# Two-layer MLP after attention, fp32 by split weights: part 2's first layer with one PSUM bank for each product and the sums on VectorE

## The chip, the cores and the metric

One Trainium2 chip, one of its cores. The metric is the device time of one execution in microseconds (us). It is given as the median of several runs; the profile shows one execution.

## What is computed

Attention with keys and values pooled by eight, then two MLPs in sequence on the 4608 tokens. The change is in the second MLP ("part 2"), whose first layer goes from 512 to 2048 units and whose second goes back to 512:

```python
def _moe_ref(x, w1, w2, w3, w_out):
    h = np.maximum(np.maximum(x @ w1, x @ w2), x @ w3)
    return h @ w_out

def _moe2_ref(x, w_in, w_out):
    h = np.maximum(x @ w_in, 0.0)
    return h * h @ w_out
```

All tensors are float32. TensorE multiplies them as pairs of parts (a high part in `float32r` and the rest), with three matmuls for each product of tiles (`PARTS`: high by high, high by rest, rest by high).

## The kernel before

Part 1 (attention and the first MLP) runs to about 764 us of the span and writes its result y to DRAM. Part 2 runs over nine blocks of 512 tokens (`for j in range(NB2)`), and in each over four groups of hidden units (`for gr in range(NG)`, 512 units each).

Both layers of part 2 are done with seven block products in place of eight, as in Strassen's scheme (Winograd's form): the operands are cut in 2 by 2 blocks, sums and differences of blocks are multiplied, and the four result blocks are sums of products. For the first layer the seven combinations of y are made and split once for each block (`mix_y`, `split_y`, L604 to L622, in the sequence of `ORDER`, L624), and the seven combinations of weights lie in SBUF (`wi2s`). `product(bank, j, gr, m)` (L639) issues the 12 matmuls of product m, 128x256 each, into one PSUM bank (6 for each half of the units, `u`). `moe2_in` (L664) forms the four unit tiles `c[h, half]` (128x512 each) from the products, and squares their positive part. With c00, c01, c10, c11 for c[0, 0] and so on, and m1 to m7 for the products, the result is

```
c00 = m1 + m2          c01 = m1 + m6 + m5 + m3
c10 = m1 + m6 + m7 + m4  c11 = m1 + m6 + m7 + m5
```

Before, three banks serve a group. Bank x takes m1, then m6, m7 and m4 on top of it, so that TensorE makes the running sums; after m1, m6 and m7 ScalarE copies the running sum out (`partial_sum`, L678), and the next product may add to the bank only when that copy has read it. m5 goes to bank y (and m3 later on top of it), m2 to bank z; VectorE adds these to the copies (`complete`, L680: an add at L656 and a square at L662). Only c10 is taken straight from bank x by ScalarE, with Relu (L698) and Square (L699).

The second layer (`moe2_out`, L765) takes the unit tiles as its left operands. For each of its products ScalarE makes the high part `g` of an operand (L124), VectorE the rest (L125), and TensorE issues 12 matmuls (L779): 8 with the high part, then 4 with the rest. They add up in five banks accA, accB, accD, accE and accF over the whole block. Groups 0 and 1 of a block have 4 such products ("outs"), groups 2 and 3 have 10 (`OUT`). When a bank is complete, `evacuate` (L737) takes it out: accA by a ScalarE copy into `o` (L748), the others by VectorE adds. An out's weights (`wo2s`, 512 KB) are fetched from DRAM shortly before, in five buffers (`wo_p`), each fetch issued by SyncE when an earlier out has released a buffer.

PSUM has eight banks: the five of `acc_ps` and three that the pool `mm_ps` hands out, the earliest released first. The order on each engine is fixed when the kernel is built: the framework's scheduler lays the instructions of all engines out by its own estimates of durations, so that outs of one group are placed between products of the next. Each engine then runs its list strictly in that order.

Of the kernel before, what the change touches and what calls it, by code (L numbers as in the profile page):

```python
# [14 lines left out]
AF = mybir.ActivationFunctionType  # L15
# [69 lines left out]
def attention_moe_kernel(ctx: ExitStack, tc: tile.TileContext, q, k, v, vn, w1, w2, w3, wo1, wi2, wo2, out):  # L85
    nc = tc.nc
# [501 lines left out]
    def shared_place(i, shape, name):  # L588
        return y_p.tile(shape, F32, tag=f"r{i}", name=name)
# [31 lines left out]
        split(y, src[m])  # L621
        src[m] = y  # L622

    ORDER = (1, 5, 6, 2, 7, 4, 3)  # L624
    early = [functools.partial(load_y, 0), functools.partial(mix_y, 0)]
    early.append(functools.partial(fetch_in, 0, w2_p))
    early += [functools.partial(split_y, 0, m) for m in ORDER]
    for i, f in enumerate(early):
# [10 lines left out]
    def product(bank, j, gr, m, first=False):  # L639

        i, o = PLACES[m]
        for u in range(2):
            n = 0
            for kk in range(2):
                for a, c in PARTS:
                    nc.tensor.matmul(  # L646
                        bank[:, u * HT : (u + 1) * HT],
                        lhsT=wi2_t[2 * gr + u][i][:, a, o + kk * P : o + (kk + 1) * P],
                        rhs=y_t[j][m][:, c, kk],
                        start=(first and u == 0 and n == 0), stop=(u == 1 and n == 5),  # L650
                        skip_group_check=not first,
                    )
                    n += 1

    def add(out, in0, in1):
        nc.vector.tensor_tensor(out=out, in0=in0, in1=in1, op=ALU.add)  # L656
# [4 lines left out]
    def squared(c):  # L661
        nc.vector.scalar_tensor_tensor(out=c, in0=c, scalar=0.0, in1=c, op0=ALU.max, op1=ALU.mult)  # L662

    def moe2_in(j, gr):  # L664

        def unit(h, half):
            if half and gr < NG // 2:
                return shared_place(4 * gr + h, [P, T2], "a21")
            return c_p.tile([P, T2], F32, tag=f"c{2 * half + h}", name=f"c{2 * half + h}")

        def bank():
            return mm_ps.tile([P, T2], F32, tag="ps", name="ps")

        c = {}

        def partial_sum(h, half, ps):
            c[h, half] = unit(h, half)
            nc.scalar.activation(c[h, half], ps, AF.Copy)  # L678

        def complete(h, half, ps):  # L680
            add(c[h, half], ps, c[h, half])
            squared(c[h, half])

        x, y = bank(), bank()
        product(x, j, gr, 1, first=True)
        partial_sum(0, 0, x)
        product(y, j, gr, 5, first=True)
        product(x, j, gr, 6)
        partial_sum(0, 1, x)
        z = bank()  # L690
        product(z, j, gr, 2, first=True)
        complete(0, 0, z)
        product(x, j, gr, 7)
        partial_sum(1, 1, x)
        complete(1, 1, y)
        product(x, j, gr, 4)
        c[1, 0] = unit(1, 0)
        nc.scalar.activation(c[1, 0], x, AF.Relu)  # L698
        nc.scalar.activation(c[1, 0], c[1, 0], AF.Square)  # L699
        product(y, j, gr, 3)  # L700
        complete(0, 1, y)
        return c

    OUT = {
        False: ((1, 0), (1, 1), (7, 1), (7, 0)),
        True: ((2, 0), (4, 1), (5, 1), (6, 1), (2, 1), (3, 1), (6, 0), (4, 0), (5, 0), (3, 0)),
    }
    BANKS = {1: "A", 2: "A", 7: "B", 4: "B", 6: "D", 5: "E", 3: "F"}
    FULL = {"A": 8, "B": 8, "D": 4, "E": 4, "F": 4}
# [86 lines left out]
    for j in range(NB2):  # L796
        for gr in range(NG):
            more = j + 1 < NB2
            c = moe2_in(j, gr)

            ready = list(ORDER) if gr == NG - 1 and more else []
            for n, (m, h) in enumerate(OUT[gr >= NG // 2]):
                if n == 6 and ready:
                    mix_y(j + 1)
                if n >= 6:
                    for y in ready[2 * n - 12 : 2 * n - 10]:
                        split_y(j + 1, y)
                moe2_out(j, gr, m, h, c)
            if gr == NG - 2 and more:
                load_y(j + 1)  # L810
            nxt = j * NG + gr + 1
            if nxt < NB2 * NG:
                fetch_group(nxt % NG)
# [41 lines left out]
```

## Time and profile before

| what | value |
|---|---|
| median of 3 runs | 1520.89 us (1520.51 to 1523.3) |
| the profiled execution: its time | 1521.12 us |
| the profiled execution: its span, first to last instruction | 1519.3 us |
| mean granted TensorE clock | 0.992 of full speed |
| busy share: TensorE matmuls, VectorE, ScalarE | 97%, 62%, 49% |
| part 2 (763.9 to 1519.3 us of the span) | 755.4 us |
| one block of part 2 away from the ends (1186.38 to 1268.61) | 82.23 us, 672 matmuls |

A reader of such a profile looks first at the engine that is busy nearly all the time, then at what ends each of its pauses. In the timeline, the bracket behind a row is the idle time of the engine before it and the instruction that ended it. Matmuls overlap each other, so the "us" of a row ends after the next row has begun; the distance from start to start is what counts.

### The profile page before, as it was taken

What the parts mean: (1) busy time and instruction counts of PE and PEld (TensorE: products, weight loads), DVE (VectorE), ACT (ScalarE), POOL (GpSimd) and SP (SyncE); (2) the same over time, 40 slices, a digit from 0 to 9 for tenths busy, and PEclk for the clock granted to TensorE, in tenths of its full rate; (3) what the DMA queues carried; (4) which work ended last, traced back from release to release, by engine and by line L of the source; (5) the groups of instructions that cost most, each with busy time, mean ns of one, the idle gap of its engine ahead of it and who ended that gap; (6) DMA issues with size and microseconds to landing.
All of it is one profiled execution on the core that took longest, in us unless ns stands there. A gap on an engine that the chain in (4) does not pass through costs nothing.

```text
span 1519.3 us, 27411 instructions
## 1 busy us (share of the span) xinstructions
PE 1467.2 (97%) x10410; PEld 1438.5 (95%) x10410; DVE 946.2 (62%) x1724; ACT 742.4 (49%) x1947; POOL 178.6 (12%) x228
## 2 busy tenths in 40 slices
PE   6879999999999999999999999999999999999998
PEld 4879999999999999999999999999999999999997
DVE  5786466675675746754335757575756657575755
ACT  6785356655666556653233434343434443443432
POOL 2442022313222212321000000000000000000000
PEclk9989999999999999999999999999999999999999
DMA  6553135534444424425197656474656566665746
GB/s 211 168 178 107 54 118 164 167 98 139 160 136 160 139 89 129 132 87 181 55 356 289 215 168 248 142 253 161 231 198 212 192 222 210 214 205 170 254 125 211
DMA packets 118306, 263.93 MB, mean 174 GB/s; under 512 B 12672, under 2 KB 62848, under 8 KB 118176
## 3 DMA queue, kind: packets, MB, share of 16 engines
q1 hardware_dynamic: 111264, 252.75, 50.3%
q10 hardware_dynamic: 6912, 9.44, 1.7%
q8 instruction: 82, 1.34, 0.4%
q14 instruction: 48, 0.39, 0.1%
HBM read 213.91 MB, written 48.23 MB: 173 GB/s over the span
## 4 chain that ended last, share of the span: by engine, by line
PE 88%; DMA 5%; ACT 4%; DVE 2%; issue 1%; SPq 0%; ACTq 0%; DVEq 0%
PE ps L502 28%; PE ps L646 23%; PE ps L521 10%; PE accB L779 6%; PE accA L779 6%; PE accE L779 3%; PE accD L779 3%; PE accF L779 3%; PE sc L342 2%; DMA wo2s<-wo_dram 2%; PE tr L370 2%; ACT ss L347 1%; PE av L399 1%; PE av L398 1%; ACT c L678 1%; DMA yr<-y_dram 1%
## 5 line engine op out<-in xcount | busy, mean ns | idle before, releaser
L502 PE MATMUL ps<-x,w 128*128 128x384 f32 x2592 | 493.6, 341 | 6.3 <-POOL w L125 4.8
L502 PEld LDWEIGHTS ps<-x,w 128*128 128x128 f32 x2592 | 451.3, 190 | 9.8 <-POOL w L125 6.4
L646 PE MATMUL ps<-y,wi2s 128*128 128x256 f32 x3024 | 388.6, 280 | 16.7 <-ACT c L678 11.1
L646 PEld LDWEIGHTS ps<-y,wi2s 128*128 128x128 f32 x3024 | 368.1, 188 | 24.0 <-ACT c L678 15.3
L521 PE MATMUL ps<-h,wo 128*128 128x384 f32 x864 | 163.2, 341 | 0.9 <-ACT ys L527 0.7
L521 PEld LDWEIGHTS ps<-h,wo 128*128 128x128 f32 x864 | 150.8, 190 | 1.7 <-ACT ys L527 0.9
L124 ACT ACTIVATE g<-c 128x512 fp32r<-128x512 f32 x144 | 90.6, 629 | 123.2 <-DVE c L662 56.7
L125 DVE TENSOR_TENSOR g<-c,g 128x512 fp32r<-128x512 f32 x144 | 99.1, 688 | 43.8 <-ACT g L124 43.1
L779 PE MATMUL accA<-wo2s,g 128*128 128x256 f32 x864 | 124.6, 283 | 1.7 <-DMA wo2s<-wo_dram 1.7
L510 DVE TENSOR_TENSOR hm<-ps,hm 128x384 f32<-128x384 f32 x144 | 79.5, 552 | 75.0 <-PE ps L502 72.7
L779 PE MATMUL accB<-wo2s,g 128*128 128x256 f32 x864 | 119.3, 283 | 0.2 <-DMA wo2s<-wo_dram 0.2
L656 DVE TENSOR_TENSOR c<-ps,c 128x512 f32<-128x512 f32 x72 | 49.5, 687 | 106.0 <-ACT c L678 90.3
L779 PEld LDWEIGHTS accA<-wo2s,g 128*128 128x128 f32 x864 | 112.3, 190 | 2.1 <-ACT g L124 1.2
L779 PEld LDWEIGHTS accB<-wo2s,g 128*128 128x128 f32 x864 | 110.4, 191 | 0.4 <-issue 0.4
L347 ACT ACTIVATE ss<-sc,st 128x72 f32<-128x72 f32 (+1 forms) x320 | 97.9, 320 | 15.1 <-DVE st L344 14.1
L353 POOL TENSOR_TENSOR ss<-ss,st 128x432 f32<-128x432 f32 (+1 forms) x64 | 56.8, 888 | 262.8 <-DVE st L352 195.9
L678 ACT ACTIVATE c<-ps 128x512 f32<-128x512 f32 x72 | 42.6, 592 | 91.5 <-PE ps L646 76.1
L656 DVE TENSOR_TENSOR a<-ps,a 128x512 f32<-128x512 f32 x36 | 24.9, 692 | 98.9 <-ACT a L678 64.5
L402 DVE TENSOR_TENSOR xf<-av,xf 64x192 f32<-64x192 f32 (+1 forms) x112 | 50.7, 453 | 48.7 <-ACT xf L401 47.1
L124 ACT ACTIVATE h<-hm 128x384 fp32r<-128x384 f32 x72 | 37.7, 523 | 73.2 <-DVE hm L510 72.6
L374 DVE TENSOR_TENSOR pt<-tr,pt 72x192 fp32r<-72x192 f32 (+1 forms) x112 | 49.7, 450 | 37.6 <-ACT pt L373 36.2
L401 ACT ACTIVATE xf<-av 64x192 f32<-64x192 f32 (+1 forms) x112 | 45.4, 405 | 54.0 <-PE av L399 39.0
(104 smaller groups left out, 2016.5 us busy)
## 6 DMA issues: line engine op xcount, KB each, us to landing
wo2s<-wo_dram SPq DMA_DIRECT2D x252, 512.0 KB, 4.6
wi2s<-wi_dram SPq DMA_DIRECT2D x24, 512.0 KB, 9.0
wraw<-in_wo_dram SPq DMA_DIRECT2D x22, 512.0 KB, 4.0
wraw<-in_w_dram SPq DMA_DIRECT2D x18, 512.0 KB, 4.2
y_dram<-ys ACTq DMA_DIRECT2D x48, 192.0 KB, 2.1
wraw<-in_wi_dram SPq DMA_DIRECT2D x16, 512.0 KB, 3.6
wi_dram<-wraw SPq DMA_DIRECT2D x16, 512.0 KB, 3.4
wo_dram<-wraw SPq DMA_DIRECT2D x64, 128.0 KB, 2.0
```

The lines of the kernel that those rows point to most:

```text
L124: nc.scalar.activation(hi, src, AF.Copy)
L125: engine.tensor_tensor(out=lo, in0=src, in1=as_f32(hi), op=ALU.subtract)
L347: nc.scalar.activation(ss[:, i, h], src[:, i, h], AF.Exp, bias=st[:, 0, i, h : h + 1], accum_out=st[:, 1, i, h : h + 1],)
L353: nc.gpsimd.tensor_tensor(out=ss, in0=ss, in1=st[:, 2].rearrange("p g (h o) -> p g h o", o=1).to_broadcast([m, g, 2, SP]), op=ALU.mult,)
L402: nc.vector.tensor_tensor(out=xf[r], in0=av[r], in1=xf[r], op=ALU.add)
L502: nc.tensor.matmul(ps, lhsT=w1_t[f, e][:, a, kk * P : (kk + 1) * P], rhs=x[kk][:, c], start=(n == 0), stop=(n == 3 * KD - 1),)
L510: nc.vector.tensor_tensor(out=hm, in0=ps, in1=hm, op=ALU.max)
L521: nc.tensor.matmul(ps, lhsT=wo1_t[kk][:, a, d * P : (d + 1) * P], rhs=hs[kk][:, c], start=(n == 0), stop=(n == 3 * KF1 - 1),)
L646: nc.tensor.matmul(bank[:, u * HT : (u + 1) * HT], lhsT=wi2_t[2 * gr + u][i][:, a, o + kk * P : o + (kk + 1) * P], rhs=y_t[j][m][:, c, kk] ...
L656: nc.vector.tensor_tensor(out=out, in0=in0, in1=in1, op=ALU.add)
L678: nc.scalar.activation(c[h, half], ps, AF.Copy)
L779: nc.tensor.matmul(bank[:, i * 256 : (i + 1) * 256], lhsT=g[:, a, u * HT + i * P : u * HT + (i + 1) * P], rhs=w[:, u, c], start=(n == 0 an ...
```

## The change

The running sums leave TensorE's banks. Each product except m3 starts in a bank of its own (m3 still goes on top of m5). ScalarE copies only m1 out; VectorE adds every other product from its bank to the unit tiles, in a chain: c01 = m6 + c00, c10 = m7 + c01, c11 = m5 + c10, then m2, m4 and m3 into c00, c10 and c01. The squares of c11 and c01 are VectorE's, those of c00 and c10 are ScalarE's, by two passes in SBUF (Relu, then Square). The products are written in the order 1, 6, 7, 5, 2, 4, 3; the parts of y are split in that order too, and out (4, 1) comes ahead of (2, 0).

```diff
-    ORDER = (1, 5, 6, 2, 7, 4, 3)
+    ORDER = (1, 6, 7, 5, 2, 4, 3)
...
+    def squared_by_scalar(c):
+        nc.scalar.activation(c, c, AF.Relu)
+        nc.scalar.activation(c, c, AF.Square)
...
-        x, y = bank(), bank()
-        product(x, j, gr, 1, first=True)
-        partial_sum(0, 0, x)
-        product(y, j, gr, 5, first=True)
-        product(x, j, gr, 6)
-        partial_sum(0, 1, x)
-        z = bank()
-        product(z, j, gr, 2, first=True)
-        complete(0, 0, z)
-        product(x, j, gr, 7)
-        partial_sum(1, 1, x)
-        complete(1, 1, y)
-        product(x, j, gr, 4)
-        c[1, 0] = unit(1, 0)
-        nc.scalar.activation(c[1, 0], x, AF.Relu)
-        nc.scalar.activation(c[1, 0], c[1, 0], AF.Square)
+        c = {(h, half): unit(h, half) for h in range(2) for half in range(2)}
+
+        def only(m):
+            ps = bank()
+            product(ps, j, gr, m, first=True)
+            return ps
+
+        nc.scalar.activation(c[0, 0], only(1), AF.Copy)
+        add(c[0, 1], only(6), c[0, 0])
+        add(c[1, 0], only(7), c[0, 1])
+        y = only(5)
+        add(c[1, 1], y, c[1, 0])
+        squared(c[1, 1])
+        add(c[0, 0], only(2), c[0, 0])
+        squared_by_scalar(c[0, 0])
+        add(c[1, 0], only(4), c[1, 0])
+        squared_by_scalar(c[1, 0])
         product(y, j, gr, 3)
-        complete(0, 1, y)
+        add(c[0, 1], y, c[0, 1])
+        squared(c[0, 1])
...
-        True: ((2, 0), (4, 1), (5, 1), (6, 1), (2, 1), (3, 1), (6, 0), (4, 0), (5, 0), (3, 0)),
+        True: ((4, 1), (2, 0), (5, 1), (6, 1), (2, 1), (3, 1), (6, 0), (4, 0), (5, 0), (3, 0)),
```

The scheduler lays out all of part 2 anew. On TensorE, the end of the products of group 1 in the third block, before: `ps_N` is a bank as the pool hands it out, `y7_` the operand of product m7, `g` that of an out.

```order
L646 MATMUL ps_10695<-y7_10464,wi2s_2_1_8541 128x256 x6
L646 MATMUL ps_10695<-y7_10464,wi2s_3_1_8549 128x256 x6
L779 MATMUL accA_10624<-wo2s_10687,g_10797 128x256 x2
L646 MATMUL ps_10695<-y4_10468,wi2s_2_1_8541 128x256 x6
L646 MATMUL ps_10695<-y4_10468,wi2s_3_1_8549 128x256 x6
L646 MATMUL ps_10696<-y3_10490,wi2s_2_3_8545 128x256 x6
L646 MATMUL ps_10696<-y3_10490,wi2s_3_3_8553 128x256 x6
```

And the same engine with the change, in the group after it in that block, from the end of the last out to the last product:

```order
L646 MATMUL ps_10967<-y7_10480,wi2s_5_1_8565 128x256 x6
L646 MATMUL ps_10981<-y5_10483,wi2s_4_2_8559 128x256 x6
L646 MATMUL ps_10981<-y5_10483,wi2s_5_2_8567 128x256 x6
L646 MATMUL ps_10996<-y2_10504,wi2s_4_0_8555 128x256 x6
L646 MATMUL ps_10996<-y2_10504,wi2s_5_0_8563 128x256 x6
L646 MATMUL ps_11012<-y4_10508,wi2s_4_1_8557 128x256 x6
L646 MATMUL ps_11012<-y4_10508,wi2s_5_1_8565 128x256 x6
L646 MATMUL ps_10981<-y3_10530,wi2s_4_3_8561 128x256 x6
L646 MATMUL ps_10981<-y3_10530,wi2s_5_3_8569 128x256 x6
```

Before, m4 adds to the bank of m7 with two matmuls in between; with the change m5, m2 and m4 have three different banks, and the bank of m5 is used again only 24 matmuls later, by m3.

On TensorE at the end of a block, around its last out into accA, before (third block into fourth):

```order
L779 MATMUL accA_10624<-wo2s_11170,g_11346 128x256 x4
L646 MATMUL ps_11488<-y5_11388,wi2s_0_2_8190 128x256 x5
L646 MATMUL ps_11488<-y5_11388,wi2s_1_2_8527 128x256 x6
L779 MATMUL accF_11070<-wo2s_11172,g_11364 128x256 x8
L779 MATMUL accD_11038<-wo2s_11174,g_11391 128x256 x8
```

And with the change, the same place:

```order
L775 MATMUL accA_10669<-wo2s_11225,g_11406 128x256 x12
L775 MATMUL accF_11125<-wo2s_11227,g_11424 128x256 x8
```

Eleven matmuls of the next block's m5 stood between the last out into accA and the next out into accF; with the change nothing stands there.

On ScalarE at that place, with the change (`o` is the copy of accA out of PSUM, `g_11424` the operand of the out into accF; before, the two stand in this order as well):

```order
L124 ACTIVATE g_11406<-c1_11239 128x512
L124 ACTIVATE y5_11471<-t5_11440 128x512
L124 ACTIVATE y7_11468<-yr_11204 128x512
L744 ACTIVATE o_11421<-accA_10669 128x512
L124 ACTIVATE g_11424<-c1_11239 128x512
L124 ACTIVATE g_11451<-s3_10897 128x512
L124 ACTIVATE g_11474<-c2_11238 128x512
```

ScalarE makes the operand of that out only after the copy of accA, which waits for the matmuls into accA.

## Rows read from the trace of the kernel before

**Rows 1.** The page's first part: engine, busy time, share of the span, instructions.

```profile
PE 1467.2 (97%) x10410; PEld 1438.5 (95%) x10410; DVE 946.2 (62%) x1724; ACT 742.4 (49%) x1947; POOL 178.6 (12%) x228
```

**Rows 2.** TensorE's waits, 763 to 1520 us: total, times, longest (us).

```profile
PE ps L646 <- ACT c L678: 11.1, 18, 1.4
PE ps L646 <- ACT a L678: 5.1, 11, 0.7
PE accA L779 <- DMA wo2s<-wo_dram: 1.7, 2, 1.0
PE accE L779 <- DMA wo2s<-wo_dram: 1.7, 1, 1.7
PE accF L779 <- ACT g L124: 1.2, 1, 1.2
```

**Rows 3.** Timeline of TensorE, one block: start, us, instruction, [idle before <-releaser].

```profile
1186.38 4.39 PE L646 MATMUL ps<-y,wi2s 128*128 128x256 f32 x36
1190.60 1.60 PE L779 MATMUL accA<-wo2s,g 128*128 128x256 f32 x12
1192.04 4.33 PE L646 MATMUL ps<-y,wi2s 128*128 128x256 f32 x36
...
1207.34 0.41 PE L779 MATMUL accA<-wo2s,g 128*128 128x256 f32 x2
1208.19 4.51 PE L646 MATMUL ps<-y,wi2s 128*128 128x256 f32 x36 [0.44 <-ACT a L678]
1212.53 1.11 PE L779 MATMUL accA<-wo2s,g 128*128 128x256 f32 x8
...
1246.63 2.40 PE L646 MATMUL ps<-y,wi2s 128*128 128x256 f32 x19
1249.71 3.09 PE L646 MATMUL ps<-y,wi2s 128*128 128x256 f32 x24 [0.69 <-ACT c L678]
1252.65 1.12 PE L779 MATMUL accB<-wo2s,g 128*128 128x256 f32 x8
...
1259.95 1.47 PE L646 MATMUL ps<-y,wi2s 128*128 128x256 f32 x11
1261.33 1.21 PE L779 MATMUL accF<-wo2s,g 128*128 128x256 f32 x8
1262.37 1.12 PE L779 MATMUL accD<-wo2s,g 128*128 128x256 f32 x8
...
1268.61 4.39 PE L646 MATMUL ps<-y,wi2s 128*128 128x256 f32 x36
```

**Rows 4.** Groups by line and shape: count | busy us, mean ns | idle before.

```profile
L662 DVE SCALAR_TENSOR_TENSOR c<-c 128x512 f32<-128x512 f32 x72 | 49.7, 690 | 1.6
L656 DVE TENSOR_TENSOR c<-ps,c 128x512 f32<-128x512 f32 x72 | 49.5, 687 | 106.0 <-ACT c L678 90.3 <-PE ps L646 15.5
L678 ACT ACTIVATE c<-ps 128x512 f32<-128x512 f32 x72 | 42.6, 592 | 91.5 <-PE ps L646 76.1 <-DVE g L125 15.4
L699 ACT ACTIVATE c<-c 128x512 f32<-128x512 f32 x36 | 22.6, 627 | 0.6
```

**Rows 5.** Timeline of TensorE, the last block's end.

```profile
1504.19 0.64 PE L779 MATMUL accA<-wo2s,g 128*128 128x256 f32 x4
1506.03 1.21 PE L779 MATMUL accF<-wo2s,g 128*128 128x256 f32 x8 [1.20 <-ACT g L124]
1507.08 1.12 PE L779 MATMUL accD<-wo2s,g 128*128 128x256 f32 x8
```

**Rows 6.** Timeline of ScalarE at that place.

```profile
1504.87 0.60 ACT L748 ACTIVATE o<-accA 128x512 f32<-128x512 f32 x1 [4.27 <-PE accA L779]
1505.36 0.62 ACT L124 ACTIVATE g<-c 128x512 fp32r<-128x512 f32 x1
```

**Rows 7.** Stretch of a block's last group: us, busy (instructions) PE PEld DVE ACT POOL, clock, DMA.

```profile
1249.70:1271.60 21.90, 21.89 (x182) 21.78 (x183) 21.51 (x36) 11.28 (x20) 0.00 (x0) 1.00 0.55 180
```

**Rows 8.** The page's DMA issues: count, KB each, median us to landing.

```profile
wo2s<-wo_dram SPq DMA_DIRECT2D x252, 512.0 KB, 4.6
```

More of the change, by code (lines that the diff above doesn't have):

```diff
@@ L672, in bank @@
             return mm_ps.tile([P, T2], F32, tag="ps", name="ps")
[L674 to L682, printed above, removed]
-        x, y = bank(), bank()
-        product(x, j, gr, 1, first=True)
-        partial_sum(0, 0, x)
-        product(y, j, gr, 5, first=True)
-        product(x, j, gr, 6)
-        partial_sum(0, 1, x)
-        z = bank()
-        product(z, j, gr, 2, first=True)
-        complete(0, 0, z)
-        product(x, j, gr, 7)
-        partial_sum(1, 1, x)
-        complete(1, 1, y)
-        product(x, j, gr, 4)
-        c[1, 0] = unit(1, 0)
-        nc.scalar.activation(c[1, 0], x, AF.Relu)
-        nc.scalar.activation(c[1, 0], c[1, 0], AF.Square)
+        c = {(h, half): unit(h, half) for h in range(2) for half in range(2)}
[13 more added lines that the diff above has]
+        squared_by_scalar(c[1, 0])
         product(y, j, gr, 3)
-        complete(0, 1, y)
+        add(c[0, 1], y, c[0, 1])
+        squared(c[0, 1])
         return c
```

## The prediction

> **What bounds the kernel now.** I read the page's engine line first: TensorE is busy 97% of the span, VectorE 62%, ScalarE 49% [rows 1]. So the time is TensorE's, and a change can move it only through the number of matmuls, their spacing, or TensorE's pauses. The number stays: 84 matmuls for the products of a group before and after. The spacing is read from the timeline: 36 matmuls of the first layer run from 1186.38 to 1190.60, 0.117 us each, and 12 of an out from 1190.60 to 1192.04, 0.120 us each [rows 3]. That leaves the pauses, so the view that matters is the list of TensorE's waits: 29 waits for a ScalarE copy out of bank x or y (L678), 16.2 us in all (11.1 + 5.1), and a few others [rows 2].
>
> The timeline shows where they fall. In the block from 1186.38 to 1268.61 there are three: 0.44 us at 1208.19, another like it 16 us later, 0.69 us at 1249.71 [rows 3]. Each is the step m7, copy, m4 in one bank. The idle time is not all of the loss: from 1207.34 to 1212.53 stand 38 matmuls, which unhindered take 2 x 0.120 + 36 x 0.117 = 4.46 us and took 5.19. The loss is 0.73 us for an idle time of 0.44. From 1246.63 to 1252.65, 43 matmuls took 6.02 us in place of 5.04: 0.98 for 0.69. So I add 0.28 us to each wait.
>
> **What goes.** The change takes away the copies between products of one bank (L678, all but the one of m1, whose bank is free again much later). The 29 waits go: 16.2 + 29 x 0.28 = **-24.3 us**.
>
> **What is added, and where it lies.** In each of the 36 groups VectorE gets eight instructions in place of six (six adds from PSUM and two squares; before, three of each), and ScalarE five as before, of which one reads PSUM in place of four. An add from PSUM takes 687 ns on VectorE and a square in SBUF 690; a ScalarE pass takes 592 from PSUM, 627 in SBUF [rows 4]. In the stretch where VectorE is fullest it ran 36 instructions in 21.51 us, 0.60 us each [rows 7]; the added 72 cost 43 us of VectorE's time. Alone on the path it would be nearly twice the gain; I cost it at nothing, and the cover is TensorE's own work. The order rows show it: m5, m2, m4 and m3 follow each other, and each needs a bank whose last product ended at least 12 matmuls (1.4 us) before. A read that TensorE waits for with nothing to do in between cost 0.98 us with a copy of 0.59; with an add of 0.69 that is 1.08, and 12 matmuls cover it. With m3 it is 24 matmuls, and the next group's m1 and m6 find banks read one or two products earlier.
>
> Only in the first block, where weights arrive in halves and six matmuls of one product alternate with six of another (0.70 us), do six matmuls not cover it: 1.08 - 0.70 = 0.4 us, at m2 in its first three groups: **+1.2 us**.
>
> If the cover fails (VectorE late by a whole add), the next thing late is m2, 0.7 us in each group it happens.
>
> Here the Trainium skill speaks against the change (Perfetto Trace Analysis, Optimizing Scalar/DVE Operations): a VectorE instruction has some 125 ns of fixed cost on PSUM and 60 on SBUF, ScalarE 51 and 93, so reading PSUM is better left to ScalarE. By it three more PSUM reads in each of 36 groups add 3 x 36 x 65 ns = 7 us (an estimate from that page) to VectorE; the trace shows 687 against 690 ns and so no such cost on VectorE, while ScalarE's 592 against 627 agrees in sign. Either way it lies beside TensorE and the sum is the same.
>
> **A new wait at each block's end.** When accA is complete, ScalarE copies it out and only then makes the operand of the next out, into accF (front section, ScalarE's order, unchanged). Before, eleven matmuls stood between the two outs: accF's began at 1261.33, after 11 matmuls from 1259.95, and those 11 and its first 8 took 2.42 us in place of 2.25. That is 0.17 us [rows 3]. With the change nothing stands between. The last block of the kernel before shows the price, because there too the outs adjoin: 4 matmuls at 1504.19, copy at 1504.87, operand at 1505.36 [rows 6], accF at 1506.03, and 12 matmuls took 2.89 us (1504.19 to 1507.08) in place of 1.44 [rows 5]. So 1.45 us, in eight more blocks: **+11.6 us**, less the seven small ones, 7 x 0.17 = **-1.2**.
>
> **Outs' weights.** Of the three waits for `wo2s` on accA and accE [rows 2], the one on accE (1.7 us, plus 0.2 for the restart) is in the last block's end. There, all ten outs now follow the last product, and the buffer it waits for is asked for four outs ahead: **-1.9**. The two on accA (1.7 us, plus 0.4) are first outs of group 3, which ran ahead of m7 and now run after m3; I take half of 2.1, **-1.0**, as such waits can come up elsewhere.
>
> Other edits cost nothing: the order of `split_y` follows the products, and out (4, 1) goes first because c11 is the first tile complete.
>
> **Sum.** -24.3 + 1.2 + 11.6 - 1.2 - 1.9 - 1.0 = -15.6 us. The profiled execution took 1521.12 us, 0.2 above the median, of which the span is 1519.3. 1521.1 - 15.6 = **1505.5 us**.
>
> **The rivals.**
> 1. *Outs' weights set the block's end.* In the last group the outs are packed: from the last matmul of the out that releases a buffer to the first that needs the refill there are 34 to 36 matmuls, 4.1 to 4.3 us, against 4.6 us from issue to landing [rows 8]. With the wait for accA's copy in between it is 5.6, so a margin of 1 us. For it: the margin is thin, and a wait on accE reached 1.7 us [rows 2]. Against: the median holds fetches that queue behind each other. If it binds, 1.0 to 1.7 us more in eight blocks: 1513 to 1519.
> 2. *accA's copy is not waited for*, because something earlier on TensorE holds the outs apart: without the +11.6, 1493 to 1494.
> 3. *The waits only change their names.* There are still three banks, and the adds form a chain; if VectorE, strictly in order, reaches m6's or m7's add late in each group, m2 and m4 wait about what m4 waited before. 28 to 36 waits of 0.7 to 1.0 us: 1518 to 1521, no change. For it: VectorE's operands from ScalarE. Against: its idle time.
> 4. *VectorE becomes the bound at the block's end (slower).* In the last group it ran without pause from 1249.70 to 1271.60 [rows 7]. With the change some 20 VectorE instructions stand between the add of m5 (2.7 us before m3 begins) and the subtraction that accF's operand needs; 20 x 0.60 = 12.1, so it is done 9.4 us after m3's beginning. accA's last matmul ends 84 matmuls after it, at 10.0 to 10.1, and its copy holds ScalarE 0.5 more [rows 6]: 10.6. The margin is 1.2 us, two instructions. Beyond it each 0.6 us costs TensorE 0.6 in eight blocks; slower than before begins where VectorE is late by 1.2 + 18.6 / 8 = 3.5 us (18.6: the sum and the 3 us a measurement can tell). If all the 43 us came to light in place of the wait at accF, 1521 - 27 + 43 = 1537. The skill's price for PSUM reads, above, would add to this one.
>
> **How the numbers follow.** A measurement of this kernel can tell about 0.2% from no change, 3 us. Chances: forecast 0.64 (faster), rival 1 0.13 (0.11 faster, 0.02 the same), rival 2 0.09 (faster), rival 3 0.08 (the same), rival 4 0.06 (slower). Faster 0.84, the same 0.10, slower 0.06. The forecast's own terms move by a few us: the first block's +1.2 may be 3, the waits for weights 0 to -4, the 1.45 us by 0.3 in eight blocks, which gives 1500 to 1510. The range takes half of rivals 1 and 2: 1496 to 1515.
>
> **What would show it.** Right: TensorE's waits for ScalarE's copies (29 before) all but gone; accF's wait for `g` at nine places of about 1.2 us idle; a block of 81.1 us in place of 82.23; VectorE's busy time up by some 45 us, ScalarE's hardly changed. Wrong: waits of the first layer's matmuls for VectorE's adds in most groups (rival 3), waits for `wo2s` on accD, accB or accE in each block (rival 1), accF's operand following VectorE's subtraction and not accA's copy (rival 4).

## The result, and the profile after

The changed kernel takes 1504.72 us (median of 4 runs, 1503.8 to 1506.67) against 1520.7 us (4 runs, 1520.01 to 1523.3): a ratio of 0.9893, 95% interval 0.9876 to 0.9911. That is faster, by 1.1%: 16.0 us where 15.4 were forecast (1505.5 us, from the median given before). The span of the profiled execution went from 1519.3 to 1502.4 us.

The page's first part answers to [rows 1]: VectorE has 44.6 us more to do, ScalarE 3.4 more, and TensorE, with as many matmuls as before, is busy 8.7 us less, in part because some of what a wait costs stands in its busy time (the prediction read 0.98 us lost for 0.69 idle).

```profile
PE 1458.5 (97%) x10410; PEld 1435.1 (96%) x10410; DVE 990.8 (66%) x1796; ACT 745.8 (50%) x1947; POOL 179.6 (12%) x228
```

TensorE's waits in part 2, all of them (engine, line, releaser: total us, times, longest), answer to [rows 2]. Not one matmul of the first layer is left in the list. What is left is the wait for `g` at the end of each of the nine blocks, 1.2 us each, and three small entries. The last of these, put down to `y`, is by the trace's DMA records a wait for weights too: they landed 0.14 us before that out began.

```profile
PE accF L775 <- ACT g L124: 10.8, 9, 1.2
PE accE L775 <- DMA wo2s<-wo_dram: 1.5, 2, 0.9
PE accB L775 <- ACT qB L738: 0.7, 1, 0.7
PE accE L775 <- ACT y L124: 0.2, 1, 0.2
```

TensorE's timeline at a block's end (columns as in [rows 3]). The out into accF begins 2.80 us after accA's twelve matmuls begin, which take 1.44; three outs on, accE waits for its weights. In the group after it 84 matmuls of the first layer run through without a pause.

```profile
1081.70 1.12 PE L775 MATMUL accD<-wo2s,g 128*128 128x256 f32 x8
1082.66 1.60 PE L775 MATMUL accA<-wo2s,g 128*128 128x256 f32 x12
1085.46 1.22 PE L775 MATMUL accF<-wo2s,g 128*128 128x256 f32 x8 [1.21 <-ACT g L124]
1086.52 1.12 PE L775 MATMUL accD<-wo2s,g 128*128 128x256 f32 x8
1087.48 1.12 PE L775 MATMUL accB<-wo2s,g 128*128 128x256 f32 x8
1089.13 1.19 PE L775 MATMUL accE<-wo2s,g 128*128 128x256 f32 x8 [0.54 <-DMA wo2s<-wo_dram]
...
1095.62 9.85 PE L646 MATMUL ps<-y,wi2s 128*128 128x256 f32 x84
```

Why accF is late stands in ScalarE's timeline at that place: the copy `o` begins when accA is complete, and `g` comes behind it, as in [rows 6]. VectorE's subtraction for that operand (second fence) had begun at 1083.09 and was done at about 1083.8, half a microsecond before the copy began.

```profile
1083.20 0.63 ACT L124 ACTIVATE y<-yr 128x512 fp32r<-128x512 f32 x1 [1.78 <-DVE yr L610]
1084.29 0.60 ACT L744 ACTIVATE o<-accA 128x512 f32<-128x512 f32 x1 [0.46 <-PE accA L775]
1084.79 0.62 ACT L124 ACTIVATE g<-c 128x512 fp32r<-128x512 f32 x1
```

```profile
1083.09 0.69 DVE L659 TENSOR_TENSOR c<-c,s 128x512 f32<-128x512 f32 x1
```

The groups by line and shape in part 2 answer to [rows 4] (count | busy us, mean ns | idle before): VectorE's adds from PSUM are now 144 and more (other forms add into `a`), at the same 688 ns; before each of them VectorE mostly waits for TensorE, not the other way round. The first layer's copies out of a bank are down to the 36 of m1.

```profile
L656 DVE TENSOR_TENSOR c<-ps,c 128x512 f32<-128x512 f32 x144 | 97.7, 688 | 72.4 <-PE ps L646 66.1 <-ACT c L685 6.0
L662 DVE SCALAR_TENSOR_TENSOR c<-c 128x512 f32<-128x512 f32 x36 | 24.8, 688 | 0.6
L665 ACT ACTIVATE c<-c 128x512 f32<-128x512 f32 x72 | 45.1, 627 | 152.6 <-DVE c L656 151.1
L685 ACT ACTIVATE c<-ps 128x512 f32<-128x512 f32 x36 | 21.4, 594 | 25.2 <-DVE g L125 13.7 <-PE ps L646 11.6
```

**Where the 16.9 us of the two profiled spans went.** For each pause in part 2 the table takes the distance from one matmul's start to the next, less 0.118 us, and adds what the matmul behind it is late, over all 6048 matmuls of part 2.

| pause in TensorE's list | before, us | after, us | difference | forecast |
|---|---|---|---|---|
| between matmuls of the first layer, or from an out into accA to them | 26.0 | 1.6 | -24.3 | -24.3 + 1.2 |
| ahead of the first out into accF at a block's end | 2.7 | 13.2 | +10.6 | +11.6 - 1.2 |
| outs that wait for weights and the like | 5.3 | 3.6 | -1.7 | -1.9 - 1.0 |
| accB in the first block, on the copy qB | 0 | 0.95 | +0.95 | none |
| sum, with rounding | 33.9 | 19.4 | -14.5 | -15.6 |

The third row holds two waits of the first block, before the change, that [rows 2] do not show, 0.2 us idle on accB and this one:

```profile
PE accF L779 <- DMA wo2s<-wo_dram: 0.4, 1, 0.4
```

Of the 26.0 us of the first row, the 29 waits for copies are 23.9. The other 2.1 are six pauses that the forecast left out: 0.9 us once, for an operand of the next block, and five of 0.1 to 0.3.

The rest of the 16.9: 0.8 us are the other matmuls' spacing, and 1.6 us lie in part 1, in which every engine runs the same sequence of instructions in both kernels: part 2's first matmul begins at 764.1 us before and at 762.5 after. Over the twelve kernels of this study that start lay between 760.8 and 764.2, so single spans differ by up to 3 us without a change in part 1's instructions.

### The profile page after: what moved, and what is told of

Its sections match the earlier page's. It is cut to its first block, busy times and chain, and to the rows that moved or that the text cites. A ratio compares the mean times of both kernels' runs of the same rounds, so it can differ in the third digit from the quotient of the medians.

```text
span 1502.4 us, 27550 instructions
## 1 busy us (share of the span) xinstructions
PE 1458.5 (97%) x10410; PEld 1435.1 (96%) x10410; DVE 990.8 (66%) x1796; ACT 745.8 (50%) x1947; POOL 179.6 (12%) x228
## 4 chain that ended last, share of the span: by engine, by line
PE 89%; ACT 4%; DMA 3%; DVE 3%; issue 1%; ACTq 0%; SPq 0%; DVEq 0%
PE ps L502 28%; PE ps L646 23%; PE ps L521 9%; PE accA L775 7%; PE accB L775 7%; PE accE L775 4%; PE accD L775 3%; PE accF L775 3%; PE sc L342 2%; PE tr L370 2%; ACT ss L347 1%; PE av L399 1%; PE av L398 1%; DMA wo2s<-wo_dram 1%; DMA vr<-in_v_dram 1%; DMA wraw<-in_w_dram 1%
## 5 line engine op out<-in xcount | busy, mean ns | idle before, releaser
L646 PE MATMUL ps<-y,wi2s 128*128 128x256 f32 x3024 | 377.9, 280 | 0.3
L656 DVE TENSOR_TENSOR c<-ps,c 128x512 f32<-128x512 f32 x144 | 97.7, 688 | 72.4 <-PE ps L646 66.1
L665 ACT ACTIVATE c<-c 128x512 f32<-128x512 f32 x72 | 45.1, 627 | 152.6 <-DVE c L656 151.1
L775 PE MATMUL accF<-wo2s,g 128*128 128x256 f32 x432 | 61.4, 285 | 10.8 <-ACT g L124 10.8
```

What stands on the lines that cost most here:

```text
L646: nc.tensor.matmul(bank[:, u * HT : (u + 1) * HT], lhsT=wi2_t[2 * gr + u][i][:, a, o + kk * P : o + (kk + 1) * P], rhs=y_t[j][m][:, c, kk] ...
L775: nc.tensor.matmul(bank[:, i * 256 : (i + 1) * 256], lhsT=g[:, a, u * HT + i * P : u * HT + (i + 1) * P], rhs=w[:, u, c], start=(n == 0 an ...
```

## The experiments

Each ratio below is against the kernel before, in runs on one chip; "lost" is reckoned as in the table.

### Is the wait at a block's end ScalarE's order alone?

```diff
-            nc.scalar.activation(o, acc, AF.Copy)
+            nc.vector.tensor_copy(out=o, in_=acc)
```

> The changed kernel, but accA's complete sum is copied into o by VectorE and not by ScalarE, so that ScalarE makes the operand g of the out into accF without waiting for accA's last matmul. In the changed kernel that out waits nine times for g, 1.2 us idle each (10.8 in all), and about 1.45 us are lost at each place. Theory A (the wait is ScalarE's order alone): the subtraction before g is done 1.0 us earlier than the copy of accA lets g begin, so 1.0 us is won at nine places, 1504.7 - 9 = 1495.7 us, and the wait for g falls to about 0.2 us idle. Theory B (the outs' weights are late next, because the out into accE already waits in six of nine blocks and everything behind accF now moves up by 1 us): most of it comes back as waits for wo2s on accB and accE, 1501 to 1503 us, and the idle time of accE for wo2s grows from 1.5 to some 7 us. I take B as the likelier.

1503.9 us (1501.6 to 1505.26), ratio 0.989 [0.9874, 0.9907]: theory B, a microsecond above its range. The wait for `g` falls from 1.2 to 0.3 us idle, and what accF loses from 13.2 to 4.5 us; accB and accE lose 11.1 us where they lost 4.3 (the first block's accB included in both). TensorE's waits:

```profile
PE accB L775 <- DMA wo2s<-wo_dram: 3.1, 5, 1.2
PE accE L775 <- DMA wo2s<-wo_dram: 2.9, 4, 1.6
PE accF L775 <- ACT g L124: 2.1, 7, 0.3
```

The wait for weights came on accB as well as on accE, where theory B had put it. ScalarE's order was the cause of the wait for `g`, and the weights stood right behind it. The 0.3 us that is left is VectorE's: the subtraction begins at 1083.96 and `g` at 1084.74, as soon as it is done.

```profile
1083.96 0.69 DVE L659 TENSOR_TENSOR c<-c,s 128x512 f32<-128x512 f32 x1
```

```profile
1084.74 0.63 ACT L124 ACTIVATE g<-c 128x512 fp32r<-128x512 f32 x1
```

### The weights in halves, alone and with the copy moved

```diff
-    wo_p = ctx.enter_context(tc.tile_pool(name="wo_p", bufs=5, reuse_waits="tile"))
+    wo_p = ctx.enter_context(tc.tile_pool(name="wo_p", bufs=11, reuse_waits="tile"))
...
-        w = wo_p.tile([P, 2, 2, 256], F32R, tag="wo2", name="wo2s")
-        nc.sync.dma_start(out=as_f32(w), in_=wo2_dram[m, gr % 2, h])
+        pair = []
+        for u in range(2):
+            w = wo_p.tile([P, 2, 256], F32R, tag="wo2", name="wo2s")
+            nc.sync.dma_start(out=as_f32(w), in_=wo2_dram[m, gr % 2, h][:, u])
+            pair.append(w)
...
```

> The changed kernel with the outs' weights fetched as two transfers of 256 KB (one for each half of the units) into eleven buffers of half the size, in place of one of 512 KB into five; so half of an out's weights may be fetched one out earlier, and only the other half has to come after the release. In the changed kernel the out into accE starts late in six blocks, 3.2 us in all. Theory A (the time from a buffer's release to landing sets this): most of these waits go, 1501.5 to 1502.5 us. Theory B (the transfers of the block's end share a bandwidth that is used up, or their number on the queue costs as much): nothing is won, 1504 to 1507 us.

1500.59 us (1499.74 to 1502.34), ratio 0.9873 [0.9858, 0.9888]: theory A. One wait for weights is left.

```profile
PE accF L778 <- ACT g L124: 10.8, 9, 1.2
PE accE L778 <- DMA wo2s<-wo_dram: 0.8, 1, 0.8
PE accB L778 <- ACT qB L741: 0.7, 1, 0.7
```

Two things changed for these weights, worked out from SyncE's issues and the trace's records of when each transfer landed. In the changed kernel the weights of that out into accE were issued 5.6 us before the out could have begun, in seven of nine blocks (at 1082.85 in the block of the timeline above). They landed 6.15 us later there, and 5.6 to 6.6 us later in the six blocks where the out is late. With halves, in six of the nine blocks, the first half was issued 6.0 to 6.2 us ahead of the out and the second 5.6 to 5.7, and both landed after 4.3 to 5.5 us. So the first half is issued half a microsecond earlier, the second hardly, and each of them lands sooner. The page's medians, 4.2 us for 512 KB and 4.3 for 256 KB, do not show that: they rest on the 27 of 252 and the 50 of 504 transfers whose landing the page could tell. Over all of them the medians are 5.0 and 4.5 us. What each part brings, and what the larger ring (eleven halves, where five wholes are ten), was not tried apart.

> Both: weights in halves, and accA's copy on VectorE. If each of the two edits removes its own wait and nothing third is late, 1504.7 - 9 - 3.2 = 1492.5 us. If the weights stay the bound of the block's end whatever the size of the transfers, 1500 to 1503 us, as with the copy on VectorE alone.

1496.66 us (1495.67 to 1497.22), ratio 0.9845 [0.983, 0.986]. In between: with both edits accF loses 4.5 us (13.2 with the halves alone) and the weights some 4 in place of 10. So each edit works. The copy's move, which alone brought 0.8 us, brings 3.9 with the halves: accF loses 8.7 us less, the outs' weights nearly 3 more.

### The step in one bank, put back

```diff
-        add(c[0, 0], only(2), c[0, 0])
+        z = only(2)
+        add(c[0, 0], z, c[0, 0])
...
-        add(c[1, 0], only(4), c[1, 0])
+        product(z, j, gr, 4, first=True)
+        add(c[1, 0], z, c[1, 0])
```

> The changed kernel, but product m4 starts again in the bank of m2, as soon as VectorE's add has read m2, so that one of the steps product, read, product in one bank is back in each of the 36 groups, with no matmul between m2 and m4. Theory A (a read by VectorE that TensorE has to wait for costs as much as the ScalarE copies did, 0.98 us for a read of 0.59, so about 1.08 for an add of 0.69): 36 waits of the first layer's matmuls for VectorE's add, 36 x 1.08 = 39 us, 1543 us. Theory B (the scheduler and the queues hide it, and separate banks are not what the change lives on): 1505 to 1515 us.

1504.1 us (2 runs, 1502.95 and 1505.25), ratio 0.9895 [0.9875, 0.9915]: a miss by 39 us for theory A, and the sentence it rested on, that nothing would stand between m2 and m4, was wrong. The scheduler put m3 and the next group's m1 there. Its list for TensorE, in one group (the operands are y_13444 for m2, y_13470 for m3, y_13397 for the next group's m1, y_13448 for m4):

```
L646 MATMUL ps<-y_13444,wi2s_0_8547 128x256 x6
L646 MATMUL ps<-y_13470,wi2s_3_8545 128x256 x6
L646 MATMUL ps<-y_13470,wi2s_3_8553 128x256 x6
L646 MATMUL ps<-y_13397,wi2s_0_8555 128x256 x6
L646 MATMUL ps<-y_13397,wi2s_0_8563 128x256 x6
L646 MATMUL ps<-y_13448,wi2s_1_8541 128x256 x6
```

So a bank that is used again costs next to nothing where 24 matmuls fit in between: one wait of 0.7 us for a VectorE add in 36 groups. The run did not test what it was built for, a bank read with nothing in between. (The wait for `g` at the nine ends of blocks is 12.3 us here, 10.8 with the change, and no out into accE waits for weights.) What costs is a read with too little work beside it, which the next two runs measure.

### The other half of the change, and the copies on the other engine

The kernel before, with the square of c00 on ScalarE:

```diff
-            squared(c[h, half])
+            if (h, half) == (0, 0):
+                nc.scalar.activation(c[0, 0], c[0, 0], AF.Relu)
+                nc.scalar.activation(c[0, 0], c[0, 0], AF.Square)
+            else:
+                squared(c[h, half])
```

> The other part alone: the kernel before with its three banks and its copies, but the square of c00 done by ScalarE in two passes. Theory A (the gain is the banks'): the waits for the copies L678 stay as they are, about 29 with 16 us idle, 1519 to 1523 us. Theory B (VectorE's relief brings part of the gain): below 1517 us.

1513.97 us (6 runs, 1511.72 to 1514.54), ratio 0.9961 [0.9949, 0.9973]. Theory B by the time, neither by the mechanism: the waits for the copies are still 29, but 12.0 us and not 16.2.

```profile
PE ps L646 <- ACT c L678: 8.8, 18, 1.4
PE ps L646 <- ACT a L678: 3.2, 11, 0.7
```

```profile
1204.28 0.65 PE L783 MATMUL accA<-wo2s,g 128*128 128x256 f32 x4
1205.13 4.51 PE L646 MATMUL ps<-y,wi2s 128*128 128x256 f32 x36 [0.20 <-ACT a L678]
```

The list was laid out anew, and between m7 and m4 now stand four matmuls of an out in place of two: 0.20 us idle where [rows 3] have 0.44. That is worth 0.24 us at each of 16 places, 3.9 of the 6 us; the others are waits of outs, which fall otherwise. VectorE's relief as such is seen nowhere: in the kernel before, TensorE waited for VectorE once in part 2, for 0.3 us.

The kernel before, with its partial sums copied by VectorE:

```diff
-            nc.scalar.activation(c[h, half], ps, AF.Copy)
+            nc.vector.tensor_copy(out=c[h, half], in_=ps)
```

> The kernel before with its banks, but the three copies of partial sums in each group are VectorE's and not ScalarE's. The step m7, copy, m4 in one bank stays; in this kernel's list m4 follows m7 with no matmul in between in some 28 of 36 groups. VectorE copied 128x512 out of PSUM in 0.694 us in the run with accA's copy on VectorE. Theory A (a read between two products of one bank is what costs, on whichever engine): 28 waits for the copy of about 0.8 us idle and 1.08 us lost each, 30 us in place of the 26 of the kernel before, 1521 to 1527 us. Theory B (what the change brings is that VectorE reads and not ScalarE, with another layout of the order as a result): 1503 to 1512 us.

1528.88 us (2 runs, 1528.07 and 1529.68), ratio 1.0057 [1.0037, 1.0077]: theory A, and 2 us worse than its range: there are 35 waits for VectorE's copies and not 28, 23.2 us in all. The seven more are short, 0.2 us idle, and come behind 60 matmuls of outs, so there it is VectorE that reaches its copy late.

```profile
PE ps L646 <- DVE c L678: 14.9, 24, 1.1
PE ps L646 <- DVE a L678: 8.3, 11, 0.8
```

```profile
1209.49 1.58 PE L646 MATMUL ps<-y,wi2s 128*128 128x256 f32 x12
1211.85 4.51 PE L646 MATMUL ps<-y,wi2s 128*128 128x256 f32 x36 [0.78 <-DVE a L678]
```

From 1209.49 to 1211.85 are 2.36 us for 12 matmuls of 0.117, so 0.95 lost, and 0.1 more in the next start. With the kernel before this makes a scale for one read between two products of a bank, reckoned as in the table: by ScalarE (0.59 us) 0.95 lost with no matmul between, 0.71 with two, 0.46 with four; by VectorE (0.69 us) 1.05 with none. Each matmul in between takes off its own 0.12 us, so by this line, an estimate, eight or nine of them hide the read. In the changed kernel, m2 of the first block has six in between and loses 0.34 to 0.41 us, as the line has it (1.05 less 0.70), and with the twelve of one product in between no wait is left, as the prediction took them.

### Does VectorE's work lie hidden?

```diff
-        squared_by_scalar(c[0, 0])
+        squared(c[0, 0])
```

and in the second run the same for c10.

> The banks alone: the changed kernel with the square of c00 on VectorE, as before the change, so that three of the four squares are VectorE's (36 more instructions there, 72 fewer on ScalarE than in the changed kernel). Theory A (VectorE's added work lies beside TensorE's; the banks bring the gain): 1504.7 us as with the change, within 2 us, VectorE's busy time up by some 25 us, no waits of the first layer for VectorE's adds. Theory B (the shift of a square to ScalarE is needed for VectorE to keep up): VectorE's 36 x 0.6 = 22 us show in part or whole, 1508 to 1526 us.

> The changed kernel with all four squares on VectorE: 72 instructions more there, as many as the change itself added, so this doubles the suspected cost. Theory A (hidden): in the block's last group the subtraction before accF's operand, which was done 1.0 us ahead of the copy of accA, comes 1.2 us later, so the out into accF loses 0.2 us more at nine places, and nothing else: 1505 to 1508 us. Theory B (rival 4 of the prediction, VectorE bounds the block's end or the groups): some 43 us of VectorE's time come to light in part or whole, 1515 to 1548 us.

Three squares: 1508.11 us (1507.93 to 1510.15), ratio 0.9935 [0.992, 0.995]. Four: 1510.05 us (1506.87 to 1512.25), ratio 0.9943 [0.9926, 0.9961]. VectorE's busy time rose by 23 and 41 us, and outside the first block no matmul of the first layer waits for VectorE. So nearly all of the work is hidden, as theory A has it; yet the times are 3 to 5 us above the changed kernel's, outside what it gave (three squares lie at the lower edge of theory B's range). Part 2 tells where, in the profiled executions against the changed kernel's (us, reckoned as in the table above):

| part 2 | three squares | four |
|---|---|---|
| first out into accF at a block's end | +3.6 | +2.1 |
| a stretch at half TensorE's clock, once and twice | +1.5 | +3.1 |
| first layer, all in the first block | +0.6 | +1.6 |
| outs' weights and the like | -2.7 | -2.2 |
| spacing of the other matmuls | +0.8 | -0.1 |
| sum, with rounding | +3.9 | +4.5 |

The first row is ScalarE's list. In seven blocks the wait for `g` grew from 1.2 to 1.7 us (14.5 us in all with three squares, 13.3 with four), though with three squares the subtraction was done as the copy of accA began. The split of an operand of the next block has slipped between the copy and `g`, 0.52 us:

```profile
1167.57 0.60 ACT L744 ACTIVATE o<-accA 128x512 f32<-128x512 f32 x1 [2.27 <-PE accA L775]
1168.07 0.62 ACT L124 ACTIVATE y<-yr 128x512 fp32r<-128x512 f32 x1
1168.59 0.62 ACT L124 ACTIVATE g<-c 128x512 fp32r<-128x512 f32 x1
```

(timeline of ScalarE, three squares on VectorE).

The second row is the clock. Behind three of the fourteen waits of 1.7 us TensorE's granted clock fell to 0.5 of full speed (1.2 GHz) for 3.4 us; the matmuls in it run 0.21 us apart in place of 0.12, and 1.5 us are lost each time. The two rows (four squares; columns as in [rows 7]) are the same stretch of two blocks, 1.5 us behind the end of such a wait:

```profile
924.30:927.70 3.40, 3.40 (x29) 3.32 (x29) 3.40 (x6) 1.19 (x3) 0.00 (x0) 1.00 0.71 257
1006.00:1009.40 3.40, 3.40 (x18) 3.40 (x18) 3.40 (x6) 1.19 (x3) 0.00 (x0) 0.50 0.69 255
```

In the profiled execution of the changed kernel, whose waits there are 1.2 us, the clock is full through part 2 until the last matmul. The executions of four squares go from 1506.87 us at a mean clock of 0.992 to 1512.25 at 0.989.

The third row is VectorE's work coming to light after all, in one place: in the first block ScalarE's copy of m1 stands behind an operand that waits for a subtraction on VectorE, and TensorE waits for the copy, 0.8 us with three squares and 1.7 with four. The banks alone, then, bring 12 of the 16 us by the medians in this layout (10 by the ratio); what the square's move adds here comes through ScalarE's list and the clock, and hardly through VectorE's time.

### A version that beats both

Weights in halves, the copy on VectorE, and the out (2, 1) third:

```diff
-        True: ((4, 1), (2, 0), (5, 1), (6, 1), (2, 1), (3, 1), (6, 0), (4, 0), (5, 0), (3, 0)),
+        True: ((4, 1), (2, 0), (2, 1), (5, 1), (6, 1), (3, 1), (6, 0), (4, 0), (5, 0), (3, 0)),
```

> Weights in halves and accA's copy on VectorE, as in the run at 1496.7 us, and in groups 2 and 3 the out (2, 1) third in place of fifth: accA is complete two outs earlier, and the operand of (2, 1), which VectorE must have read before it may overwrite c10 with the difference for accF, is made earlier. In the run at 1496.7 us the out into accF still loses 0.5 us at each of nine places (4.5 us), with the subtraction now the last thing before g. Theory A (the subtraction waits only for its place in VectorE's list, which is now three instructions, 1.8 us, earlier): that 4.5 goes, 1492 to 1493 us. Theory B (the weights, which still cost 3.7 us there, take over, as what follows accF moves up by 0.5 us): 1494 to 1497 us.

1494.7 us (1493.32 to 1496.14), ratio 0.9847 [0.9831, 0.9863]: theory B. The wait for `g` is gone from the list (0.3 us is still lost at the last block's end), and accE waits for its weights (6.4 us lost in seven blocks).

```profile
PE accE L778 <- DMA wo2s<-wo_dram: 4.8, 4, 1.7
PE accB L778 <- ACT qB L741: 0.7, 1, 0.7
```

Then the same with the halves cut otherwise, by part (high or rest) and not by units; part 1 stores the weights in that order, too:

```diff
...
-        for u in range(2):
+        for c in (1, 0):
             w = wo_p.tile([P, 2, 256], F32R, tag="wo2", name="wo2s")
-            nc.sync.dma_start(out=as_f32(w), in_=wo2_dram[m, gr % 2, h][:, u])
-            pair.append(w)
+            nc.sync.dma_start(out=as_f32(w), in_=wo2_dram[m, gr % 2, h][:, c])
+            pair[c] = w
...
-                        rhs=w[u][:, c], start=(n == 0 and k == 0),
+                        rhs=w[c][:, u], start=(n == 0 and k == 0),
```

> The kernel of 1494.7 us (weights in halves, accA's copy on VectorE, out (2, 1) third), but the two halves of an out's weights are now its two parts: the rest part, which is read by matmuls 5 to 8 of the out's 12 alone, is fetched first, and so an out's high part waits for the release of a rest part, which comes four matmuls sooner, and in this order of outs often 1 to 2 us sooner. In the run at 1494.7 us the out into accE still waits for its weights in seven blocks, 6.4 us lost. Theory A (the release sets it): these go, 1488 to 1489.5 us. Theory B (the transfers of the block's end share a bandwidth that is used up, ten outs' weights of 512 KB in 15 us): the wait moves on to the next out, 1493 to 1496 us.

1490.53 us (1489.34 to 1491.63), ratio 0.9807 [0.9791, 0.9824]: theory A, a microsecond above its range. One wait for weights remains in the list, and TensorE loses 4.5 us in the whole of part 2 (33.9 before, 19.4 with the change):

```profile
PE accE L778 <- DMA wo2s<-wo_dram: 0.9, 1, 0.9
PE accB L778 <- ACT qB L741: 0.7, 1, 0.7
```

## Why the prediction was right, step by step

- **The 29 waits (-24.3) and the first block (+1.2).** Right: -24.3 together against -23.1, where the 29 waits gave 23.9 and pauses that were not forecast another 1.6. The first block does lose time in its first three groups, each time at m2 (768.70, 784.59 and 795.07), which begins 0.2 to 0.3 us late behind VectorE's add of m6: 1.1 us with the late starts. These waits are too short for the list. The reading of 0.28 us per wait beyond its idle time was needed: the idle times alone (16.2 us) would have made the gain 8 us smaller. The run with four matmuls between and the one with copies on VectorE give the same scale.
- **accF's wait (+11.6, -1.2).** Right in place, cause, count and size: nine places, 1.21 us idle, 1.47 us lost each where 1.45 was read from the last block [rows 5]. The copy moved to VectorE took 8.8 of the 13.2 us away.
- **VectorE's added work at nothing.** Right: 44.6 us more busy, and no wait of the first layer for it outside the first block, not with another 41 us either; in the first block those brought 1.6 us to light. The margin at accF was about 1 us, as the count of twenty instructions gave (subtraction done at 1083.8, end of the copy's hold on ScalarE 1084.8). The sentence on the Trainium skill stands as it was put (Perfetto Trace Analysis, Optimizing Scalar/DVE Operations): an add that reads PSUM took VectorE 688 ns in the changed kernel and a square in SBUF 688 or 690, so no run here shows the 65 ns between the two that the page's figures make.
- **Outs' weights (-2.9).** Too good by 1.2 us. The waits of the kernel before did go, but the out into accE now starts late in six of nine blocks, 3.2 us in all. This is rival 1 in a small form: it set the start of one out by 0.1 to 1.1 us, not 1.0 to 1.7 us in eight blocks. The step that was off is the landing time. The weights were asked for 5.6 us ahead, as forecast, but the 4.6 us set against it is a median over all fetches; these took 5.6 to 6.6 us in the six late blocks, where before the change they took 3.3 to 4.7 in every block but the last, and 7.3 there, with the outs packed. The margin of 1 us was not there.
- **"Other edits cost nothing."** Not quite: with out (4, 1) first, in the first block the last out of group 1 into accB and the first of group 2 into accB adjoin, and the copy qB lies between them, 0.95 us:

```profile
806.52 3.04 PE L775 MATMUL accB<-wo2s,g 128*128 128x256 f32 x24
810.25 1.69 PE L775 MATMUL accB<-wo2s,g 128*128 128x256 f32 x12 [0.69 <-ACT qB L738]
```

  It is the very pattern that the change removes elsewhere: an out, a ScalarE copy and an out in one bank.
- **The block of 81.1 us.** From one accF to the next the blocks took 79.9 (the last), and 81.07 to 82.24 us, median 81.4; the shortest full ones, without a wait for weights, 81.07 and 81.10.
- **What the sum hides.** Weights and accB cost 2.2 us more than forecast and accF 0.2, the first layer lost 1.2 less, and the spacing gave 0.8: the errors nearly cancel. So the mechanism was right, and that the number came within a microsecond is in part luck. And one thing the prediction did not weigh: that the list itself is laid out anew brings some microseconds of either sign, 6 us for moving one square alone.

Open: why the scheduler leaves two matmuls or none between m7 and m4 in the kernel before, and finds 24 in the run with m4 in the bank of m2, was not tried apart; the run with copies on VectorE shows only that the reading engine does not settle it.

## What to carry to other kernels

Price a read between two uses of one accumulator by what stands between them in the engine's list: here 0.95 us with nothing, 0.12 less for each matmul, nothing from one product of twelve on; a bank of its own is one way to get a product in between, an order that puts other work there is another. Where TensorE is busy 97% of the time, taking away one wait can show the next right behind it (here the weights behind the copy), so look at what is second before costing the gain. Set a margin against the landing times of the fetches it is for, not against a median over all. When an edit changes the instructions that a scheduler lays out, compare the lists around the waits before giving the edit itself the credit.

## What the runs showed that was not expected

Half the bytes took only a tenth less time from issue to landing: 4.5 us for 256 KB, 5.0 for 512 KB, medians over all transfers of outs' weights. The granted clock fell to half for 3.4 us behind three of fourteen waits of 1.7 us. A VectorE copy of 128x512 out of PSUM took 694 ns where ScalarE took 592 to 594. And two shifts in the lists, neither of them work that was added, were worth nearly 4 us each: one ScalarE pass slipped between a copy and an operand (3.6 us at accF), and two more matmuls in a gap (3.9 us).
